# Attention by 64x64 tiles inside an MLP on one core: heads 0 and 2, 1 and 3 put in one tile, states applied in two parts with the scores between them

## The chip, the core and the metric

The kernel runs on one core of one Trainium2 chip. The metric is the device time of one execution in microseconds. TensorE (PE) does the matrix multiplications; each is a weight load (PEld in the profile) and a matmul that streams the other operand past the weights into a bank of PSUM. VectorE (DVE), ScalarE (ACT) and GpSimd (POOL) do elementwise work, and SyncE (SP) issues most of the DMAs.

## The reference

A decayed linear attention over blocks of 64 positions feeds an MLP with a quick GELU. Cut to what matters:

```python
batch, n_heads, seq, head_dim = (4, 8, 768, 64);  block = 64
for b in range(nb):
    intra = np.einsum('bhic,bhjc->bhij', qb, kb) * Dmask[None]       # scores
    intra = np.einsum('bhij,bhjd->bhid', intra, vb)
    inter = np.einsum('bhid,bhde->bhie', qb * lam_pow[None], kv_state)
    out[:, :, sl] = intra + inter                                    # mix
    kv_state = lam_block * kv_state + np.einsum('bhsd,bhse->bhde', kb * rev_pow, vb)
x = out.transpose(0, 2, 1, 3).reshape(B * S, H * D)                  # 3072 x 512
h = x @ w_in                                                         # d_ff 2048
return ((h * (1.0 / (1.0 + np.exp(-1.702 * h)))) @ w_out)            # 3072 x 512, f32
```

## The kernel before

The work is cut into six waves of 512 tokens. Waves 0 and 1 hold the first 256 positions of two batch rows each and are made by separate functions (`big_...`). Waves 2 to 5 hold 128 positions, two blocks of 64, of all four batch rows, and are what the change is about.

Each wave goes through the MLP in 32 items of four 128x512 matmuls each: 16 calls of `mlp1` (line 434, a GELU on ScalarE behind each) and 16 of `mlp2` (line 447), four for each 128 rows of output; a copy (line 451, VectorE) and a store on SyncE follow the fourth. The last 128 rows of the last wave are done by `mlp2_part` (line 458) in column pieces, each with its own copy (line 461) and store.

The order is written out by hand. `main` is the list of MLP items; `side` holds the pieces of attention with the index of the item ahead of which they are issued. While wave w goes through the MLP, the attention of wave w+1 is put between its items, counted from the wave's first item n. Each engine works its own instructions in the order of issue. Attention in waves 2 to 5 goes by pairs of heads p = 0 to 3:

- `load` asks for q, k and v of the wave after next, 24 DMAs of 128 KB on SyncE's queue, at item 8.
- `do_cast` (items 1, 3, 5, 7) multiplies k and q by their powers into a bf16 tile (lines 220 and 221, VectorE), casts v (line 223, GpSimd) and issues a transposing DMA on SyncE's queue (line 226). A tile holds the two heads of a pair, 2p and 2p+1, side by side.
- `scores` (line 376, 64x64 matmuls) for two pairs at once, followed by the mask on VectorE (line 379).
- `state_mm` (line 390, 64x64) and `state_up` (line 399, VectorE): the state after the first block goes to `half_sb`, that after the second to `kv_sb`. Such a state tile is 128x128 for each batch row, with the two heads' 64x64 states on the diagonal and zeros beside them, which `state_zeros` writes on GpSimd.
- `mix` applies the states (line 412, 128x64 matmuls with the block-diagonal state as weights), adds the masked scores times v (line 418, 64x64) and copies the result to xT on ScalarE (line 422). With `then` it also issues scores and states of two other pairs behind its own matmuls.

A 64x64 matmul uses one quarter of the array, a tile set by the half of the input partitions (rows) and the half of the output partitions (columns). `quads` lists the four combinations so that each four neighbours lie on four tiles:

```python
quads = [(r, slice(64 * r, 64 * r + 64), h, slice(64 * h, 64 * h + 64)) for r in range(2) for h in range(2)]
```

PSUM has two groups of banks in this kernel: three of tag "mm" for the MLP and five of tag "att" for attention (`bank`); scores with `spare` take one from "mm". A bank is given out again once its last reader is done.

Of the kernel before, what the change touches and what calls it, by code (L numbers as in the profile page):

```python
# [24 lines left out]
def kernel(  # L25
# [50 lines left out]
    def load(w):  # L76
        for g in range(2):
            for nm in "kqv":
                loaded[w, nm, g] = ld.tile([P, B, 4, D], f32, tag=f"{nm}{g}", name=f"{nm}f")
            for hd in range(4 * g, 4 * g + 4, 2):  # L80
                for nm, src in (("k", k), ("q", q), ("v", v)):
                    for h in (hd, hd + 1):
                        nc.sync.dma_start(
                            out=loaded[w, nm, g][:, :, h % 4, :],
                            in_=src[:, h, w * P : (w + 1) * P, :].rearrange("b s d -> s b d"))
# [84 lines left out]
    def late_pows():  # L170
        for h in range(2):
            hs = slice(64 * h, 64 * h + 64)
            nc.gpsimd.tensor_copy(blk_pow[hs], l64[hs].rearrange("p (n h) -> p n h", h=2)[:, :, h])
        nc.gpsimd.tensor_tensor(blk2_pow, blk_pow, blk_pow, op=MUL)
# [4 lines left out]
    def state_zeros(tiles):  # L179
        for x in tiles:  # L180
            nc.gpsimd.memset(x, 0.0)
# [32 lines left out]
    def do_cast(w, p):  # L214
        kf, qf, vf = (pair_of(w, nm, p) for nm in "kqv")
        kqs = work.tile([P, 2, B, 2, D], bf16, tag=f"kqs{p}", name="kqs")
        ks, qs = kqs[:, 0], kqs[:, 1]
        for h in range(2):
            hd = 2 * p + h
            nc.vector.tensor_scalar(ks[:, :, h, :], kf[:, :, h, :], scalar1=k_pow[:, hd : hd + 1], scalar2=None, op0=MUL)  # L220
            nc.vector.tensor_scalar(qs[:, :, h, :], qf[:, :, h, :], scalar1=q_pow[:, hd : hd + 1], scalar2=None,  # L221
                                    op0=MUL)
        nc.gpsimd.tensor_copy(v_sb[w % 2][p], vf)  # L223
        cast[w, p] = kqs.rearrange("p i b h d -> p i b (h d)")
# [96 lines left out]
    def big_st(w, p0):  # L321
        first, second = part_sb[p0 // 2]
        for i in range(2):
            p = p0 + i
            nc.gpsimd.tensor_scalar(first[:, i], first[:, i], scalar1=blk2_pow[:, p : p + 1], scalar2=None, op0=MUL)  # L325
            for h in range(2):
                hs = slice(64 * h, 64 * h + 64)
                nc.gpsimd.tensor_tensor(kv_sb[0][p][hs, BB * w : BB * w + BB, hs], first[hs, i], second[hs, i], op=ADD)  # L328
# [39 lines left out]
    quads = [(r, slice(64 * r, 64 * r + 64), h, slice(64 * h, 64 * h + 64)) for r in range(2) for h in range(2)]  # L368

    def scores(w, pairs, spare=False):  # L370
        s2 = [bank([P, 2, B, D], f32, "ps_s", spare and h == 0) for h in range(2)]
        for i, p in enumerate(pairs):
            kq = trans[w, p]
            for b in range(B):
                for r, rs, h, hs in quads:
                    nc.tensor.matmul(s2[h][rs, i, b, :], kq[hs, 0, b, rs], kq[hs, 1, b, rs], start=True, stop=True)  # L376
        for h in range(2):
            sm = work.tile([P, 2, B, D], bf16, tag="sm", bufs=8, name="sm")
            nc.vector.tensor_tensor(sm, s2[h], mask_pow[:, pairs[0] : pairs[0] + 2, h, None, :].to_broadcast([P, 2, B, D]),  # L379
                                    op=MUL)  # L380
            masked[w, pairs[0], h] = sm

    def state_mm(w, pairs):
        nr = 2 if w + 1 < NW else 1
        ps_kv = [bank([P, 2, B, D], f32, f"ps_kv{r}") for r in range(nr)]
        for i, p in enumerate(pairs):
            ks, vt = cast[w, p][:, 0], v_sb[w % 2][p]
            for b in range(B):
                for r, rs, h, hs in quads[: 2 * nr]:
                    nc.tensor.matmul(ps_kv[r][hs, i, b, :], ks[rs, b, hs], vt[rs, b, h, :], start=True, stop=True)  # L390
        return ps_kv

    def state_up(w, pairs, ps_kv):
        for r, kv in enumerate(ps_kv):
            for i, p in enumerate(pairs):
                old, new = (kv_sb[w % 2][p], half_sb[p]) if r == 0 else (half_sb[p], kv_sb[(w + 1) % 2][p])
                for h in range(2):
                    hs = slice(64 * h, 64 * h + 64)
                    nc.vector.scalar_tensor_tensor(new[hs, :, hs], old[hs, :, hs], blk_pow[hs, p : p + 1], kv[hs, i],  # L399
                                                   op0=MUL, op1=ADD)  # L400

    def attend(w, pairs):
        scores(w, pairs)
        state_up(w, pairs, state_mm(w, pairs))

    def mix(w, pairs, then=()):
        ps_o = [bank([P, 2, B, D], f32, f"ps_o{r}") for r in range(2)]
        for i, p in enumerate(pairs):
            for r in range(2):
                kv = half_sb[p] if r else kv_sb[w % 2][p]  # L410
                for b in range(B):
                    nc.tensor.matmul(ps_o[r][:, i, b, :], kv[:, b, :], trans[w, p][:, 1, b, r * D : r * D + D],  # L412
                                     start=(i == 0 and b == 0), stop=False, skip_group_check=True)
        for i, p in enumerate(pairs):
            vt = v_sb[w % 2][p]
            for b in range(B):
                for r, rs, h, hs in quads:
                    nc.tensor.matmul(ps_o[r][hs, i, b, :], vt[rs, b, h, :], masked[w, pairs[0], h][rs, i, b, :],  # L418
                                     start=False, stop=True, skip_group_check=True)
# [195 lines left out]
```

## Time and profile before

| | us |
|---|---|
| median of 3 runs | 210.43 (210.26 to 210.76) |
| profiled execution | 210.89 |
| its span in the trace | 209.2 |
| TensorE busy | 199.2 (95%) |
| VectorE busy | 96.8 (46%) |
| ScalarE busy | 86.7 (41%) |
| GpSimd busy | 49.0 (23%) |

Times in the profile are microseconds from the span's start unless ns is written. A group's line gives source line, engine, operation, output and inputs, shape and count, then busy time, mean ns of one, and the idle time of the engine before them with what ended it. A stretch's line gives start and end, its length, the busy time and number of instructions of PE, PEld, DVE, ACT and POOL, TensorE's granted clock, the DMA engines' busy share and GB/s. A timeline line gives start, length, engine, line, operation and count of merged neighbours; in brackets stands idle time before them. A chain line gives start (in the timeline's sense), length and what ran, or only length and share where it is summed.

### The profile page before, as it was taken

How to read it: one execution, taken by the hardware profiler on the slowest of the kernel's cores; microseconds unless marked ns; L12 is line 12 of the kernel's file. 1: busy time of each engine (PE TensorE's matmuls, PEld its weight loads, DVE VectorE, ACT ScalarE, POOL GpSimd, SP SyncE). 2: the span in 40 equal slices, each digit the busy share in tenths (PEclk: the TensorE clock that was granted, in tenths of full speed). 3: DMA queues.
4: the chain of work that ended last, by engine and by line, in shares of the span. 5: the costliest groups of instructions: out<-in, count | busy, mean ns of one | idle time of the engine just before them, and what ended most of it. 6: DMA issues, size and time to landing. Idle time of an engine off the chain costs nothing.

```text
span 209.2 us, 5215 instructions
## 1 busy us (share of the span) xinstructions
PE 199.2 (95%) x2167; PEld 104.6 (50%) x2195; DVE 96.8 (46%) x215; ACT 86.7 (41%) x159; POOL 49.0 (23%) x99
## 2 busy tenths in 40 slices
PE   7979999999999988999999999999999999999993
PEld 7745444555444454444545444545444545444462
DVE  3886000568960399634692725692815251100121
ACT  4539762165766022365212465202466202565000
POOL 4279986183790011200211001111000000000000
PEclk9999999999999999999999999999999999999999
DMA  5999999999999998999993399884490011100112
GB/s 172 267 239 206 198 203 237 297 272 206 189 287 183 201 228 185 279 193 208 209 201 134 90 179 225 183 178 168 98 158 0 34 69 54 50 0 0 53 54 96
DMA packets 88237, 33.89 MB, mean 162 GB/s; under 512 B 68630, under 2 KB 85270, under 8 KB 88214
## 3 DMA queue, kind: packets, MB, share of 16 engines
q1 hardware_dynamic: 83174, 28.98, 60.6%
q0 software_dynamic: 4224, 4.19, 12.4%
q10 hardware_dynamic: 816, 0.39, 0.6%
q8 instruction: 17, 0.28, 0.6%
q14 instruction: 6, 0.05, 0.1%
HBM read 27.26 MB, written 6.29 MB: 160 GB/s over the span
## 4 chain that ended last, share of the span: by engine, by line
PE 83%; DMA 7%; DVE 4%; issue 2%; ACT 2%; ACTq 0%; POOL 0%; POOLq 0%
PE ps_h L434 39%; PE ps_out L447 35%; DMA vb<-in_v_dram 5%; DVE half L399 2%; DMA qb<-in_q_dram 2%; PE ps_part L458 2%; PE ps_o L412 1%; PE ps_o L418 1%; PE ps_s L376 1%; DVE sm L379 1%; DVE kv L399 1%; PE ps_kv L390 1%; ACT mid L315 1%; PE ps_o L348 1%; ACT L555 1%
## 5 line engine op out<-in xcount | busy, mean ns | idle before, releaser
L434 PE MATMUL ps_h<-xT,w_in 128*128 128x512 bf16 x372 | 84.1, 379 | 0.8 <-issue 0.2
L447 PE MATMUL ps_out<-w_out,g_sb 128*128 128x512 bf16 x355 | 80.4, 379 | 1.8 <-issue 1.6
L437 ACT ACTIVATE g_sb<-ps_h 128x512 bf16<-128x512 f32 x96 | 57.1, 598 | 41.8 <-PE ps_h L434 41.7
L434 PEld LDWEIGHTS <-w_in 128*128 128x128 bf16 x384 | 37.1, 98 | 44.5 <-DVE xT L359 0.3
L447 PEld LDWEIGHTS <-g_sb 128*128 128x128 bf16 x368 | 35.0, 98 | 40.6
L451 DVE COPY o_sb<-ps_out 128x512 f32<-128x512 f32 x19 | 13.1, 692 | 55.1 <-PE ps_out L447 53.3
L223 POOL CAST v_sb<-vf 128x512 bf16<-128x512 f32 x16 | 10.1, 638 | 73.2 <-DMA vf<-in_v_dram 62.1
L422 ACT CAST xT<-ps_o 128x512 bf16<-128x512 f32 x16 | 8.6, 590 | 44.0 <-PE ps_o L418 37.4
L379 DVE TENSOR_TENSOR sm<-ps_s,mask_pow 128x512 bf16<-128x512 f32 x16 | 10.3, 686 | 21.5 <-PE ps_s L376 21.4
L399 DVE SCALAR_TENSOR_TENSOR half<-kv,blk_pow,ps_kv 64x256 bf16<-64x256 bf16 x32 | 15.3, 478 | 0.7
L251 DVE TENSOR_TENSOR kqb<-kb,kb_pow 128x256 bf16<-128x256 f32 x10 | 3.9, 422 | 21.4 <-DMA kb<-in_k_dram 19.0
L221 DVE TENSOR_SCALAR kqs<-qf,q_pow 128x256 bf16<-128x256 f32 x32 | 12.6, 395 | 0.8 <-DMA qf<-in_q_dram 0.8
L220 DVE TENSOR_SCALAR kqs<-kf,k_pow 128x256 bf16<-128x256 f32 x32 | 12.1, 377 | 0.5 <-DMA kf<-in_k_dram 0.4
L289 DVE SCALAR_TENSOR_TENSOR smb<-ps_s,inv_pow,mask_b 128x512 bf16<-128x512 f32 x16 | 11.0, 745 | 2.3 <-PE ps_s L281 2.3
L399 DVE SCALAR_TENSOR_TENSOR kv<-half,blk_pow,ps_kv 64x256 bf16<-64x256 bf16 x24 | 11.5, 480 | 0.8
L328 POOL TENSOR_TENSOR kv<-part,part 64x128 bf16<-64x128 f32 x16 | 7.4, 461 | 1.2
L239 PEld LDWEIGHTS <-warm 128*128 128x128 bf16 x79 | 5.8, 127 | 2.0 <-DVE warm L105 1.2
L239 PE MATMUL fill<-warm 128*128 128x64 bf16 (+2 forms) x61 | 5.6, 272 | 1.2 <-DVE warm L105 1.2
L325 POOL TENSOR_SCALAR part<-part,blk_pow 128x128 f32<-128x128 f32 x8 | 5.2, 644 | 5.0 <-ACT part L319 4.4
L268 PEld LDWEIGHTS <-kqb 128*128 128x128 bf16 x64 | 4.5, 105 | 2.8 <-DVE kqb L251 1.5
L451 ACT COPY o_sb<-ps_out 128x512 f32<-128x512 f32 x4 | 2.3, 586 | 8.2 <-PE ps_out L447 8.2
L251 DVE TENSOR_TENSOR kqb<-qb,qb_pow 128x256 bf16<-128x256 f32 x13 | 5.6, 458 | 0.2
(78 smaller groups left out, 123.9 us busy)
## 6 DMA issues: line engine op xcount, KB each, us to landing
out_dram<-o_sb SPq DMA_DIRECT2D x23, 256.0 KB, 2.8
kf<-in_k_dram SPq DMA_DIRECT2D x32, 128.0 KB, 3.4
qf<-in_q_dram SPq DMA_DIRECT2D x32, 128.0 KB, 3.9
vf<-in_v_dram SPq DMA_DIRECT2D x32, 128.0 KB, 3.5
vb<-in_v_dram SPq DMA_DIRECT2D x8, 256.0 KB, 5.5
w_in<-in_moe_w_in_dram POOLq DMA_DIRECT2D x4, 512.0 KB, 9.3
w_out<-in_moe_w_out_dram POOLq DMA_DIRECT2D x4, 512.0 KB, 14.9
kb<-in_k_dram SPq DMA_DIRECT2D x8, 128.0 KB, 3.7
```

Of the source, the lines that this page charges most:

```text
L220: nc.vector.tensor_scalar(ks[:, :, h, :], kf[:, :, h, :], scalar1=k_pow[:, hd : hd + 1], scalar2=None, op0=MUL)
L221: nc.vector.tensor_scalar(qs[:, :, h, :], qf[:, :, h, :], scalar1=q_pow[:, hd : hd + 1], scalar2=None, op0=MUL)
L223: nc.gpsimd.tensor_copy(v_sb[w % 2][p], vf)
L239: nc.tensor.matmul(dst, warm[:, :P], warm[:, : dst.shape[1]], start=True, stop=True, skip_group_check=True)
L251: eng.tensor_tensor(x[:, bb].rearrange("p t (h d) -> p h t d", h=2), pair_of(w, nm, p)[:, bb], by, op=MUL)
L289: nc.vector.scalar_tensor_tensor(sm.rearrange("p b t s -> p b (t s)"), s2.rearrange("p b t s -> p b (t s)"), inv_pow[:, 2 * p + h : 2 * p ...
L379: nc.vector.tensor_tensor(sm, s2[h], mask_pow[:, pairs[0] : pairs[0] + 2, h, None, :].to_broadcast([P, 2, B, D]), op=MUL)
L399: nc.vector.scalar_tensor_tensor(new[hs, :, hs], old[hs, :, hs], blk_pow[hs, p : p + 1], kv[hs, i], op0=MUL, op1=ADD)
L434: nc.tensor.matmul(h_ps[fc], w_in_sb[j][:, kc, i * P : (i + 1) * P], xT[w, kc], start=(kc == 0), stop=(kc == KC - 1))
L437: nc.scalar.activation(g_of[w][:, fc, :], h_ps.pop(fc), GELU)
L447: nc.tensor.matmul(ps_out, g_of[w][:, fc, g * P : (g + 1) * P], w_out_sb[j][:, fc % CW, :], start=(fc == 0), stop=(fc == FFC - 1))
L451: (nc.scalar.copy if w == 0 else nc.vector.tensor_copy)(o, ps_out)
```

## The change

For waves 2 to 5, a tile of q and k now holds heads 0 and 2, or 1 and 3, of a group of four (loads, casts and the powers follow that). A head's v stays where it was. The states become 64 columns wide, without zero blocks: heads 2i+j of a group sit in tile j, partitions 64i to 64i+63; `state_zeros` goes, and a state update covers 128 partitions in one instruction. The states are applied by 64x64 matmuls in two parts: `mix_first` with the two halves of the input partitions writing to swapped banks, `mix_rest` with them straight, followed by the masked scores times v. Between the parts stand the scores and states of two other tiles (`mix_attend`) or four small matmuls of zeros (`mix`); `in_turn` issues one of them. Pieces are placed anew: waves 4 and 5 have their first two pairs cast and scored two MLP waves ahead instead of one, and their loads go out in two halves. The last block's columns go in three pieces of 256, 128 and 128.

```diff
-    def load(w):
-        for g in range(2):
+    def load(w, gs=(0, 1)):
+        for g in gs:
...
-            for hd in range(4 * g, 4 * g + 4, 2):
+            for j in range(2):
                 for nm, src in (("k", k), ("q", q), ("v", v)):
-                    for h in (hd, hd + 1):
+                    for h in ((2 * j, 2 * j + 1) if nm == "v" else (j, j + 2)):
...
-    kv_sb = [[const.tile([P, B, P], bf16, name=f"kv{i}{p}") for p in range(NP)] for i in range(2)]
-    half_sb = [const.tile([P, B, P], bf16, name=f"half{p}") for p in range(NP)]
+    kv_sb = [[const.tile([P, B, D], bf16, name=f"kv{i}{p}") for p in range(NP)] for i in range(2)]
+    half_sb = [const.tile([P, B, D], bf16, name=f"half{p}") for p in range(NP)]
...
+    half_of = [slice(0, D), slice(D, P)]
+    quads = [(i, half_of[i], j, half_of[j]) for i in range(2) for j in range(2)]
+
+    def score_mm(w, p0, spare=False):
         s2 = [bank([P, 2, B, D], f32, "ps_s", spare and h == 0) for h in range(2)]
-        for i, p in enumerate(pairs):
-            kq = trans[w, p]
-            for b in range(B):
-                for r, rs, h, hs in quads:
-                    nc.tensor.matmul(s2[h][rs, i, b, :], kq[hs, 0, b, rs], kq[hs, 1, b, rs], start=True, stop=True)
+        for b in range(B):
+            for r in range(2):
+                for i, rows, j, _ in quads:
+                    kq, rs = trans[w, p0 + j], half_of[r]
+                    nc.tensor.matmul(s2[i][rs, j, b, :], kq[rows, 0, b, rs], kq[rows, 1, b, rs], start=True, stop=True)
...
+    def state_mm(w, p0):
...
+                for r, rs, i, rows in quads[: 2 * nr]:
+                    nc.tensor.matmul(ps_kv[r][rows, j, b, :], cast[w, p0 + j][rs, 0, b, i, :],
+                                     v_sb[w % 2][p0 + i][rs, b, j, :], start=True, stop=True)
...
-                for h in range(2):
-                    hs = slice(64 * h, 64 * h + 64)
-                    nc.vector.scalar_tensor_tensor(new[hs, :, hs], old[hs, :, hs], blk_pow[hs, p : p + 1], kv[hs, i],
-                                                   op0=MUL, op1=ADD)
+                nc.vector.scalar_tensor_tensor(new, old, blk_pow[:, p : p + 1], ps_kv[r][:, j], op0=MUL, op1=ADD)
+
+    def in_turn():
+        nc.tensor.matmul(bank([P, W], f32, "turn")[:D, :D], warm[:D, :D], warm[:D, :D], start=True, stop=True)
...
+    def mix_old(w, p0, swapped):
+        for b in range(B):
+            for i, rows, j, cols in quads:
+                r, p = (1 - i if swapped else i), p0 + j
                 kv = half_sb[p] if r else kv_sb[w % 2][p]
-                for b in range(B):
-                    nc.tensor.matmul(ps_o[r][:, i, b, :], kv[:, b, :], trans[w, p][:, 1, b, r * D : r * D + D],
-                                     start=(i == 0 and b == 0), stop=False, skip_group_check=True)
+                nc.tensor.matmul(mix_of[w, p0][r][cols, i, b, :], kv[rows, b, :], trans[w, p][rows, 1, b, half_of[r]],
+                                 start=(swapped and b == 0), stop=False, skip_group_check=True)
...
+    def mix(w, p0):
+        mix_first(w, p0)
+        for _ in range(4):
+            in_turn()
+        mix_rest(w, p0)
+
+    def mix_attend(w, p0, w2, p2):
+        mix_first(w, p0)
+        in_turn()
+        attend(w2, p2, True)
+        if w2 + 1 == NW:
+            in_turn()
+        mix_rest(w, p0)
...
-                    + [(mlp2_part, w, G - 1, c0, d_model // 2) for c0 in (0, d_model // 2)])
+                    + [(mlp2_part, w, G - 1, c0, n) for c0, n in ((0, 2 * P), (2 * P, P), (3 * P, P))])
...
-                side += [(n + 1 + 2.0 * p, (do_cast, w + 1, p)) for p in range(NP)]
-                at = (21, 25, 28) if w == 1 else (13, 20, 27)
-                side += [(n + at[0], (attend, w + 1, [0, 1])), (n + at[1], (mix, w + 1, [0, 1], (w + 1, [2, 3]))),
-                         (n + at[2], (mix, w + 1, [2, 3]))]
-            if w and w + 2 < NW:
-                side += [(n + 8, (load, w + 2))]
+                p0, ahead = (2 if w > 2 else 0), w > 1 and w + 2 < NW
+                side += [(n + 1 + 2.0 * (p - p0), (do_cast, w + 1, p)) for p in range(p0, NP)]
+                if w < 3:
+                    side += [(n + (20 if w == 1 else 13), (attend, w + 1, 0))]
+                side += [(n + (25 if w == 1 else 18 if w == 2 else 13), (mix_attend, w + 1, 0, w + 1, 2))]
+                if ahead:
+                    side += [(n + (8 if w == 2 else 5), (load, w + 2, (0,))), (n + 21, (load, w + 2, (1,)))]
+                    side += [(n + 15 + 1.5 * p, (do_cast, w + 2, p)) for p in range(2)]
+                    side += [(n + 27, (mix_attend, w + 1, 2, w + 2, 0))]
+                else:
+                    side += [(n + 28, (mix, w + 1, 2))]
+                if w == 1:
+                    side += [(n + 8, (load, w + 2))]
```

Left out here: `do_cast` and `late_pows` index heads and powers by the new places, `big_st` writes its result there, `mix_rest` multiplies the masked scores by v with each four neighbours on four tiles, as before.

More of the change, by code (lines that the diff above doesn't have):

```diff
@@ L416, in mix, with mix_rest @@
+    def mix_rest(w, p0):
+        ps_o = mix_of[w, p0]
+        mix_old(w, p0, False)
+        for i in range(2):
             for b in range(B):
[L417 to L420 removed]
+                for r, rs, j, cols in quads:
+                    nc.tensor.matmul(ps_o[r][cols, i, b, :], v_sb[w % 2][p0 + i][rs, b, j, :],
+                                     masked[w, p0 + i][rs, j, b, :], start=False, stop=True, skip_group_check=True)
+        x = x_tile(w, p0).rearrange("p i (b r s) -> p r (i b) s", b=B, r=2)
@@ L550 @@
         late_mask()
-        state_zeros(kv_sb[0])
         late_pows()
```

75 lines of the change are left out of this document (31 added, 44 removed).

## The prediction

> **What bounds the kernel now.** I read the page first, then the groups of instructions, the stretches (one for each wave of the MLP), and last the timeline of TensorE around the attention pieces.
>
> ```profile
> span 209.2 us, 5215 instructions
> PE 199.2 (95%) x2167; PEld 104.6 (50%) x2195; DVE 96.8 (46%) x215; ACT 86.7 (41%) x159; POOL 49.0 (23%) x99
> ```
>
> ```profile
> L434 PE MATMUL ps_h<-xT,w_in 128*128 128x512 bf16 x372 | 84.1, 379 | 0.8 <-issue 0.2
> L447 PE MATMUL ps_out<-w_out,g_sb 128*128 128x512 bf16 x355 | 80.4, 379 | 1.8 <-issue 1.6
> ```
>
> ```profile
> L434 PEld LDWEIGHTS <-w_in 128*128 128x128 bf16 x384 | 37.1, 98 | 44.5 <-DVE xT L359 0.3 <-issue 0.3
> L447 PEld LDWEIGHTS <-g_sb 128*128 128x128 bf16 x368 | 35.0, 98 | 40.6
> ```
>
> TensorE is busy 95% of the span and no other engine over 46%. The groups also show that the trace lacks records: 384 weight loads stand against 372 matmuls on L434, 368 against 355 on L447. I must allow for that when I read gaps.
>
> ```profile
> 147.28 6.47 PE ps_h L434 x30
> ```
>
> ```profile
> 85.30:116.20 30.90, 30.48 (x349) 15.42 (x352) 17.49 (x40) 11.72 (x20) 3.29 (x5) 1.00 0.86 200
> 116.20:147.10 30.90, 30.48 (x349) 15.40 (x352) 17.13 (x40) 11.71 (x20) 2.46 (x4) 1.00 0.75 171
> 147.10:177.90 30.80, 30.38 (x317) 15.29 (x320) 13.30 (x32) 11.72 (x20) 0.00 (x0) 1.00 0.33 70
> ```
>
> The chain of waits gives the pace of the large matmuls: 6.47/30 = 0.2157 us. A wave has 128 of them, 27.61 us. These three stretches, MLP waves 2 to 4 at full clock (1.00), take 30.90, 30.90 and 30.80 us, so the attention of the next wave adds 3.29, 3.29 and 3.19 us to each on TensorE. That, and the same in wave 1, is all that the change can act on before the tail; work moved on the other engines counts only where TensorE waits for it.
>
> **What one attention piece costs now.** A wave has three: scores and states of heads 0 to 3 (`attend`); the mix of those followed by scores and states of heads 4 to 7; the mix of the latter. In the timeline the first column is the start.
>
> ```profile
> 96.08 0.59 PE L434 MATMUL ps_h<-xT,w_in 128*128 128x512 bf16 x2
> 96.60 0.45 PE L376 MATMUL ps_s<-kqT 64*64 64x64 bf16 x32
> 96.88 0.46 PE L390 MATMUL ps_kv<-v_sb,kqs 64*64 64x64 bf16 x32
> 97.27 0.82 PE L434 MATMUL ps_h<-xT,w_in 128*128 128x512 bf16 x2
> ```
>
> ```profile
> 103.32 0.28 PE L412 MATMUL ps_o<-kqT,kv 128*128 128x64 bf16 x4
> 103.44 0.28 PE L412 MATMUL ps_o<-kqT,half 128*128 128x64 bf16 x4
> ```
>
> ```profile
> 103.88 0.45 PE L418 MATMUL ps_o<-sm,v_sb 64*64 64x64 bf16 x32
> 104.16 0.49 PE L376 MATMUL ps_s<-kqT 64*64 64x64 bf16 x32
> 104.47 0.50 PE L390 MATMUL ps_kv<-v_sb,kqs 64*64 64x64 bf16 x32
> 105.12 0.38 PE L447 MATMUL ps_out<-w_out,g_sb 128*128 128x512 bf16 x1 [0.16 <-issue]
> ```
>
> ```profile
> 111.51 0.45 PE L418 MATMUL ps_o<-sm,v_sb 64*64 64x64 bf16 x32
> 112.11 4.26 PE L447 MATMUL ps_out<-w_out,g_sb 128*128 128x512 bf16 x19 [0.16 <-issue]
> 116.22 1.46 PE L434 MATMUL ps_h<-xT,w_in 128*128 128x512 bf16 x6
> ```
>
> Entry into 64x64 tiles: 96.08 plus two paces is 96.51, and the scores start at 96.60: 0.09 us. Thirty-two small matmuls of which four neighbours lie on four different tiles: 96.60 to 96.88, or 103.88 to 104.16: 0.28 us, 0.035 for each round of four. The way back: five calls, 20 matmuls, stand between 112.11 and 116.22, yet only 19 are recorded, and 4.11/0.2157 is 19, so the first is the missing one and truly started at 111.90. After L418's 0.28 us that leaves 0.11 us, and the "0.16 issue" is no stall. The attend piece agrees: 97.27 - 96.88 = 0.39 = 0.28 + 0.11. L412's sixteen 128x64 matmuls with the switch behind them take 103.88 - 103.32 = 0.56 us, 0.12 for each four (103.44 - 103.32).
>
> So attend costs 0.09 + 0.28 + 0.28 + 0.11 = 0.76, the mix 0.56 + 0.28 + 0.11 = 0.95, the middle piece 0.56 + 3 x 0.28 + 0.11 = 1.51 (1.57 in the rows, with the same missing record). Their sum, 3.22 to 3.28, is the 3.29 of the stretches.
>
> In wave 1 there are stalls besides:
>
> ```profile
> 76.66 0.22 PE L390 MATMUL ps_kv<-v_sb,kqs 64*64 64x64 bf16 x2
> 77.25 0.44 PE L390 MATMUL ps_kv<-v_sb,kqs 64*64 64x64 bf16 x30 [0.38 <-DVE kv L399]
> 77.85 2.54 PE L447 MATMUL ps_out<-w_out,g_sb 128*128 128x512 bf16 x11 [0.16 <-issue]
> ```
>
> ```profile
> 80.46 0.28 PE L412 MATMUL ps_o<-kqT,kv 128*128 128x64 bf16 x4
> 81.22 0.29 PE L412 MATMUL ps_o<-kqT,half 128*128 128x64 bf16 x4 [0.49 <-DVE half L399]
> ```
>
> From 76.66 to 77.25 less a pair's 0.02 is 0.57 us; from 80.46 to 81.22 less 0.12 is 0.64. Wave 1 thus pays 3.29 + 1.21 = 4.50, and all four waves 14.27 us.
>
> **The change, part by part.**
>
> *States applied as 64x64 tiles.* Sixteen 128x64 matmuls and a switch (0.56) become 32 small ones, each four on four tiles: 2 x 0.14 = 0.28. With the entry that a mix did not have (0.09) a mix saves 0.19.
>
> *Scores.* This speaks against the change. In the old loop four neighbours went to four tiles. The new loop nests rows, then input half, then pair, with the output's partitions set by the rows: each two neighbours fall on the same tile, A A B B C C D D. The rows of the old kernel show what one tile can do where the states of the last wave use only two tiles:
>
> ```profile
> 158.71 0.42 PE L390 MATMUL ps_kv<-v_sb,kqs 64*64 64x64 bf16 x16
> 159.06 0.82 PE L434 MATMUL ps_h<-xT,w_in 128*128 128x512 bf16 x2
> ```
>
> 159.06 - 158.71 - 0.11 = 0.24 us for eight pairs: a tile takes a new matmul every 0.030 to 0.035 us however few share the array. If matmuls start in the order of the program, A's second waits one such time, B starts with it, B's second waits again: four times per eight matmuls instead of two. Thirty-two then take 16 x 0.034 = 0.55 us, not 0.28: +0.27 for each of eight score steps, 2.2 us in all. The bounds are 0 (if the engine passed over the waiting one) and, were a second weight load also exposed, twice that. I take 0.27, nearest to the two-tile row.
>
> The Trainium skill, "TensorE: Matmul & The Clock Gate", Part 3 (packing small matmuls), says that matmuls start and end strictly in program order; by it the scores cost the 0.55 and the sum below holds; without it they could cost 0.28 (rival 1). No row here shows it either way.
>
> ```profile
> L390 PE MATMUL ps_kv<-v_sb,kqs 64*64 64x64 bf16 x224 | 3.9, 194 | 0.4 <-DVE kv L399 0.4
> L399 DVE SCALAR_TENSOR_TENSOR half<-kv,blk_pow,ps_kv 64x256 bf16<-64x256 bf16 x32 | 15.3, 478 | 0.7
> L379 DVE TENSOR_TENSOR sm<-ps_s,mask_pow 128x512 bf16<-128x512 f32 x16 | 10.3, 686 | 21.5 <-PE ps_s L376 21.4
> ```
>
> *Fewer pieces, and the turns.* The time between the two halves of a mix is filled by scores and states, or, where there are none, by four `in_turn` matmuls. After the change there are two attends, six joint pieces and two lone mixes: ten visits instead of twelve. Costs: attend 0.09 + 0.55 + 0.28 + 0.11 = 1.03. Joint: 0.09 + 0.14 + 0.03 (one turn) + 0.55 + 0.28 + 0.14 + 0.28 + 0.11 = 1.62 (two of them with half the states, 0.24 + a turn, about the same). Lone mix: 0.09 + 0.14 + 0.14 + 0.28 + 0.11 = 0.76 plus the turns. Four on one tile take 4 x 0.03 = 0.13; but the fourth reuses the first one's bank and waits for its end, 0.19 us after its start by the mean of L390's 64x64 matmuls: 0.25 us with the wait's own time, between 0.13 and 0.8 if every turn waited so. A lone mix is 1.01. Sum: 2 x 1.03 + 6 x 1.62 + 2 x 1.01 = 13.80 us without stalls, against 14.27: -0.47.
>
> *VectorE, and wave 1's stall.* Fifty-six state updates of 64x256 become 28 of 128x256, the same free size, so 0.48 us each: 13 us less of VectorE, off the path in waves 2 to 4. In wave 1 the last mix needs, through a turn's bank, all of two masks and four updates: 2 x 0.69 + 4 x 0.48 = 3.3 us after the scores. The scores now stand ahead of the rest of their own mix, so TensorE has 0.28 + 0.14 + 0.28 + 0.11 of that piece, twelve large matmuls (2.59) and 0.23 of the next piece, 3.6 us, before it asks; the output copy that stood before the masks (the call before) is done by then. So I cost the stall at nothing, with 0.3 us to spare; if that cover goes, up to 1.21 comes back. Next late would be xT's copy, with 16 large matmuls before it is read.
>
> *Moved casts, loads, transposes.* Casts of the wave after next (pairs 0 and 1) go to items 15 and 16.5, half of the loads to item 8 or 5, the other to 21. On SyncE twelve loads now stand ahead of two transposes, and twelve behind one output store. Before, TensorE never waited on these in waves 2 to 4 and VectorE worked 17.5 of 30.9 us. The casts read what was asked for seven items (6 us) before; twelve loads of 128 KB at the stretch's 200 GB/s take 7.9 us, so VectorE may wait some 2 us there with the next masks queued behind. But the states that follow those masks are wanted nine items (7.8 us) after their scores, and masks and updates take 3.3. Cost 0, up to 1 us if loads land later still. The zeroing of twelve state tiles on GpSimd goes; it was waited for nowhere: 0.
>
> *Last block in three.*
>
> ```profile
> 204.05 0.42 DVE L461 COPY o_part<-ps_part 128x256 f32<-128x256 f32 x1 [1.05 <-PE ps_part L458]
> ```
>
> ```profile
> 202.27 3.51 PE ps_part L458 x32
> ```
>
> ```profile
> 46.77 0.22 PE ps_tk L268 x4
> ```
>
> ```profile
> out_dram<-o_sb SPq DMA_DIRECT2D x23, 256.0 KB, 2.8
> out_dram<-o_part SPq DMA_DIRECT2D x2, 128.0 KB, 1.7
> L451 DVE COPY o_sb<-ps_out 128x512 f32<-128x512 f32 x19 | 13.1, 692 | 55.1 <-PE ps_out L447 53.3
> ```
>
> On TensorE 16 x 0.110 (3.51/32) become 32 x 0.055 (0.22/4): nothing. The last copy shrinks: 0.69 for 512 columns, 0.42 for 256, hence 0.29 for 128: -0.13. The last store lands sooner: 2.8 to 1.7 for half the bytes bounds it at 0 to -0.5; I take -0.12. Tail: -0.25.
>
> **Sum.** -0.47 - 0.25 = -0.7 us. The profiled execution took 210.89 us (209.2 span and 1.7 around it), 0.46 above the median of 210.43; so 210.2 for it and 209.7 for the median. About 0.2% (0.42 us) is what a measurement can tell from no change.
>
> **The rivals.**
> (1) The array hides the paired order: scores stay at 0.28. For it: weight loads run ahead. Against: two-tile rows show each tile at its limit, and no row shows a later matmul starting first. -0.7 - 2.2 = -2.9: 207.5.
> (2) Slower: the second of two neighbours on one tile also waits for its weights, because loads into rows in use are not hidden. Place: 128 such followers in the eight score steps; price up to a tile's 0.032 us each, 4.1: 213.8. It decides from 0.7/128 = 0.006 us on. Against: L412's neighbours all use the whole array and still follow at 0.03 (0.12/4), loads hidden. The same section of the Trainium skill states in a list that a load overlaps running matmuls only when its row group differs (the text above the list allows a background weight buffer too); by the list's rule this rival would hold, but the L412 rows, each on the rows of its forerunner, disagree.
> (3) The stall of wave 1 stays (0.3 us is little), or moved loads land late: -0.7 + 1.2 = +0.5: 210.9.
>
> **How the numbers follow.** Forecast 58%, rival 1 14%, rival 2 14%, rival 3 14%. The forecast's own range: the pair's time between 0.030 and 0.035 (+-0.3), turns and tail (+-0.3): 209.1 to 210.4; it is faster by over 0.2% in most of it, 50 of its 58. With rival 1's 14: 0.64. Same: 8 of the forecast, 4 of rival 3: 0.12. Slower: rival 2 and the rest of rival 3: 0.24. The range, 207.3 to 211.0, takes in rivals 1 and 3 and leaves out rival 2.
>
> **What would show it.** Scores of 32 taking 0.55 (0.28: rival 1; 0.8 or more: rival 2); 64x64 state rows of 0.14 per 16; waves 3 and 4 at about 30.8 and 30.2 us, wave 2 longer, near 31.9, since it gets a third piece; no releaser "DVE" before TensorE in wave 1 (rival 3 if there); a last copy of 0.29. Waves 2 to 4 all above 31 would make the prediction wrong.

## The result, and the profile after

The changed kernel takes 209.17 us (median of seven runs), the kernel before beside it 210.76 (seven runs): ratio 0.9913, 95% interval 0.9886 to 0.9940, so 1.8 us less (1.3 to 2.4). The ratio is one of means and leaves out one execution of the changed kernel, of 213.72 us, that fell in a slower state. On record stood a forecast of -0.7 (209.7, range 207.3 to 211.0) and, as rival 1, -2.9. The result is faster, as forecast, and lies halfway between the two, so some term of the sum must be wrong. The profiled execution took 209.56 us.

Two lines of the page (the profile's summary) after:

```profile
span 207.9 us, 5498 instructions
PE 198.2 (95%) x2327; PEld 102.3 (49%) x2355; DVE 82.2 (40%) x188; ACT 86.5 (42%) x159; POOL 45.2 (22%) x88
```

VectorE lost 14.6 us of work (96.8 before) and GpSimd 3.8; TensorE is as full as it was. The stretches of MLP waves 2 to 4 of the changed kernel, from each wave's first weight load to the next one's:

```profile
84.89:116.25 31.36, 30.94 (x448) 15.57 (x451) 17.55 (x46) 11.70 (x20) 4.69 (x5) 1.00 0.96 200
116.25:146.66 30.41, 30.09 (x369) 14.83 (x372) 12.27 (x30) 11.61 (x20) 2.74 (x5) 1.00 0.86 197
146.66:176.67 30.01, 29.80 (x308) 14.31 (x311) 6.94 (x16) 11.61 (x20) 0.62 (x1) 1.00 0.21 59
```

They were forecast at near 31.9, 30.8 and 30.2, against 30.9, 30.9 and 30.8 before. Now one attend piece of wave 2:

```profile
95.24 1.24 PE L451 MATMUL ps_h<-xT,w_in 128*128 128x512 bf16 x5
96.42 0.46 PE L377 MATMUL ps_s<-kqT 64*64 64x64 bf16 x32
96.69 0.48 PE L389 MATMUL ps_kv<-v_sb,kqs 64*64 64x64 bf16 x32
97.11 1.04 PE L451 MATMUL ps_h<-xT,w_in 128*128 128x512 bf16 x3
```

The scores take 96.42 to 96.69, 0.27 us, where 0.55 was forecast: rival 1's sign. The joint piece of wave 3, which has half the states, shows how it can be (a count of x1 stands for single matmuls):

```profile
141.74 0.41 PE L389 MATMUL ps_kv<-v_sb,kqs 64*64 64x64 bf16 x14
141.96 0.22 PE L411 MATMUL ps_o<-kqT,half 64*64 64x64 bf16 x2
141.98 0.20 PE L389 MATMUL ps_kv<-v_sb,kqs 64*64 64x64 bf16 x2
142.01 0.19 PE L411 MATMUL ps_o<-kqT,half 64*64 64x64 bf16 x1
142.01 0.19 PE L398 MATMUL turn<-warm 64*64 64x64 bf16 x1
...
142.10 0.19 PE L424 MATMUL ps_o<-sm,v_sb 64*64 64x64 bf16 x1
142.11 0.19 PE L411 MATMUL ps_o<-kqT,kv 64*64 64x64 bf16 x1
```

In the program all sixteen L389 come first, then the turn (L398), then all L411 of `mix_rest`, then L424. In the trace two L411 start at 141.96, ahead of the last L389 at 141.98 and of the turn at 142.01, and an L424 at 142.10 ahead of an L411 at 142.11. The states here are those of the last wave and use one half of the input partitions; the L411 that pass them, those of `half`, use the other. TensorE lets a later small matmul on a free tile start before an earlier one that waits.

Could the program itself stand in another order than the source? The kernel sets its order by hand (`tc.manual_schedule()`), and the same calls in wave 4 run in a slightly different one, with thirteen L389 ahead of the two L411 instead of fourteen:

```profile
158.65 0.38 PE L389 MATMUL ps_kv<-v_sb,kqs 64*64 64x64 bf16 x13
158.84 0.22 PE L411 MATMUL ps_o<-kqT,half 64*64 64x64 bf16 x2
```

The table gives what the pieces cost, each as the time from the start of the last large matmul ahead to that of the first one behind, less the pace of 0.2157 us for each (the missing record behind a piece allowed for):

| us | before | forecast | after |
|---|---|---|---|
| attend | 0.76 | 1.03 | 0.785 |
| joint piece, waves 1 and 2 | 2.12 (stalled) and 1.58 | 1.62 | 1.47 |
| joint piece, waves 3 and 4 | 1.50 to 1.56 | 1.62 | 1.34 to 1.43 |
| lone mix, wave 4 | 0.95 | 1.01 | 1.01 |
| lone mix, wave 1 | 1.61 | 1.01 | 1.21 |
| all of waves 1 to 4 | 14.23 | 13.80 | 12.34 |
| last matmul to the end | 3.41 | 3.16 | 3.10 |

Pieces and tail together are 2.2 us less. The span is only 1.3 less, because the first large matmul (its weight load) started at 19.42 instead of 18.58. Nothing ties that to the change: in the other profiles this start lies between 18.03 and 19.71 whichever kernel it is, the old order's own at 18.41, 18.58 and 19.71.

### The profile page after: what moved, and what is told of

It is laid out like the page before. It is cut to its first block, busy times and chain, and to the rows that moved or that the text cites. A ratio compares the mean times of both kernels' runs of the same rounds, so it can differ in the third digit from the quotient of the medians.

```text
span 207.9 us, 5498 instructions
## 1 busy us (share of the span) xinstructions
PE 198.2 (95%) x2327; PEld 102.3 (49%) x2355; DVE 82.2 (40%) x188; ACT 86.5 (42%) x159; POOL 45.2 (22%) x88
## 4 chain that ended last, share of the span: by engine, by line
PE 87%; DMA 7%; ACT 2%; issue 1%; SPq 0%; POOL 0%; ACTq 0%; DVE 0%; POOLq 0%
PE ps_h L451 39%; PE ps_out L464 38%; DMA vb<-in_v_dram 5%; PE ps_part L475 2%; DMA qb<-in_q_dram 2%; PE ps_o L411 2%; PE ps_o L424 1%; PE ps_s L377 1%; PE ps_kv L389 1%; ACT mid L314 1%; PE ps_o L348 1%; ACT L571 1%; PE ps_kv L307 1%; PE ps_s L280 1%; PE ps_tq L267 0%
## 5 line engine op out<-in xcount | busy, mean ns | idle before, releaser
L222 POOL CAST v_sb<-vf 128x512 bf16<-128x512 f32 x16 | 11.7, 740 | 74.9 <-DMA vf<-in_v_dram 74.8
L395 DVE SCALAR_TENSOR_TENSOR half<-kv,blk_pow,ps_kv 128x256 bf16<-128x256 bf16 x16 | 6.9, 473 | 0.0
L250 DVE TENSOR_TENSOR kqb<-qb,qb_pow 128x256 bf16<-128x256 f32 x13 | 6.2, 504 | 0.1
L267 PEld LDWEIGHTS <-kqb 128*128 128x128 bf16 x64 | 4.0, 98 | 3.7 <-DVE kqb L250 2.6
L268 ACT COPY kqB<-ps_tq 128x512 bf16<-128x512 bf16 x6 | 3.5, 586 | 5.1 <-PE ps_tq L267 5.1
## 6 DMA issues: line engine op xcount, KB each, us to landing
w_out<-in_moe_w_out_dram POOLq DMA_DIRECT2D x4, 512.0 KB, 14.6
```

The source lines that it names most:

```text
L222: nc.gpsimd.tensor_copy(v_sb[w % 2][p], pair_of(w, "v", p))
L250: eng.tensor_tensor(x[:, bb].rearrange("p t (h d) -> p h t d", h=2), pair_of(w, nm, p)[:, bb], by, op=MUL)
```

## The experiments

Each ratio is to the kernel before on the same chip, with its 95% interval. The cost of a piece is read from the run's profile as in the table above. For all four orders of the score loop: eight score steps lie in the pieces, and the rest of the kernel is the changed one.

### The order of the scores on the tiles

**Four neighbours on four tiles (s_four).**

```diff
-        for b in range(B):
-            for r in range(2):
-                for i, rows, j, _ in quads:
...
+        for b in range(B):
+            for j in range(2):
+                for r in range(2):
+                    for i in range(2):
...
```

> The changed kernel with the score loop nested so that each four neighbours lie on four tiles, as in the old kernel; nothing else differs. Theory A (mine on record: matmuls start in order, and a tile takes one per 0.032 us) needs the paired order to cost 0.55 us for 32 scores; the new trace already shows the first 32 in 0.27, so A is in trouble, and if its records' starts hid a cost this kernel would be 2 us faster than the changed one. Theory B (the array takes two matmuls per half of its rows every 0.032 us, whichever columns they use): no difference, 0.27 to 0.28 us for 32 scores, total within 0.3 us of the changed kernel.

Measured: ratio 0.9914 (0.9883 to 0.9945), attend 0.762 against 0.785. The paired order costs 0.02 in an attend piece, nothing in the joint pieces (1.47 in both) and nothing that the time can tell. Going back to the old kernel's order of tiles brings nothing, so nothing was lost by leaving it.

**Sixteen on one row half (s_half).**

```diff
+        for i in range(2):
+            for b in range(B):
+                for j in range(2):
+                    for r in range(2):
...
```

> The changed kernel with the score loop's outermost index the half of the input partitions: 16 scores in a row on one half of the rows, alternating between its two tiles, then 16 on the other. Theory A (one matmul per tile per 0.032 us): 16 pairs of 0.032, 0.51 us for 32 scores instead of 0.27, so 8 x 0.24 = 1.9 us slower than the changed kernel. Theory B (two per row half per 0.032): the same 0.51 us and +1.9 us. Theory C (only the rate of issue, about 0.008 us for each matmul, sets the pace): 0.27 us and no difference.

**Eight on one tile (s_tile).**

```diff
+        for i in range(2):
+            for r in range(2):
+                for b in range(B):
+                    for j in range(2):
...
```

> The changed kernel with 8 scores in a row on the same tile, tile after tile. Theory A (one per tile per 0.032 us, in order): 32 x 0.032 = 1.0 us for 32 scores, 8 x 0.75 = 6 us slower than the changed kernel. Theory B (two per row half per 0.032 us whichever columns): 0.51 us, 1.9 us slower. Theory C (issue alone): no difference.

Measured: s_half 0.9949 (0.9922 to 0.9976), attend 0.874, that is +0.11 over s_four; s_tile 1.0039 (1.0011 to 1.0068), attend 1.174, +0.41, and the whole of the change's gain is lost by a loop order alone. None of the three theories fits: over s_four's, all pieces together cost 0.57 us more in s_half (on record 1.9 or nothing) and 2.97 in s_tile (on record 6, 1.9 or nothing). In s_tile's attend:

```profile
96.79 0.80 PE L378 MATMUL ps_s<-kqT 64*64 64x64 bf16 x29
97.40 0.22 PE L390 MATMUL ps_kv<-v_sb,kqs 64*64 64x64 bf16 x3
97.43 0.19 PE L378 MATMUL ps_s<-kqT 64*64 64x64 bf16 x1
97.45 0.20 PE L390 MATMUL ps_kv<-v_sb,kqs 64*64 64x64 bf16 x2
...
97.49 0.19 PE L378 MATMUL ps_s<-kqT 64*64 64x64 bf16 x1
```

The states, which stand behind all scores in the program, start at 97.40, before the scores are through. In strict order, four runs of eight on one tile would take at least four times seven steps of 0.032, 0.90 us, from first to last start, and the states would follow; the last score starts at 97.49, 0.70 us after the first, with some of the states already under way.

**Four on one tile (s_quad).**

```diff
+        for b2 in range(0, B, 2):
+            for r in range(2):
+                for i in range(2):
+                    for b in (b2, b2 + 1):
+                        for j in range(2):
...
```

> The changed kernel, with the score loop so that each four neighbours fall on one tile (A A A A B B B B C C C C D D D D, twice). Measured so far per attend piece over four neighbours on four tiles (0.762): pairs on one tile +0.02, sixteen on one row half +0.11, eight on one tile +0.41. Theory one, strict order of the program with 0.032 us for each follower on a tile: +0.57 per piece, eight pieces 4.6 us, ratio 1.013. Theory two, TensorE looks past a waiting matmul at about the next four: +0.12 per piece (worked out step by step with one start in 0.008 us and 0.032 us per tile), 1.0 in all, ratio 0.996. Theory three, it looks past eight or more: +0.03 or less, ratio 0.991 to 0.992.

Measured: 0.9947 (0.9917 to 0.9977), attend 0.832, +0.07; the joint pieces rose by 0.04. Strict order (+0.57) is refuted. How many matmuls TensorE looks past is not settled. An estimate worked out step by step, with one start in 0.008 us (0.27/32) and 0.032 us between two on one tile, gives 0, 0.03, 0.13 and 0.19 for pairs, fours, a row half and eights with a look-ahead of eight, and 0, 0.13, 0.19 and 0.38 with one of four; measured are 0.02, 0.07, 0.11 and 0.41. What limits the look-ahead stays open.

### Where the gain comes from

**Same tiles, old number of pieces (n_ahead).**

```diff
...
+                side += [(n + 1 + 2.0 * p, (do_cast, w + 1, p)) for p in range(NP)]
+                at = (20, 25, 28) if w == 1 else (13, 20, 27)
+                side += [(n + at[0], (attend, w + 1, 0)), (n + at[1], (mix_attend, w + 1, 0, w + 1, 2)),
+                         (n + at[2], (mix, w + 1, 2))]
+            if w and w + 2 < NW:
+                side += [(n + 8, (load, w + 2))]
```

> The changed kernel, but with the pieces of attention placed as the old order has them: in each of MLP waves 1 to 4 one attend, one joint piece and one lone mix, casts at items 1, 3, 5, 7 and loads at item 8. Twelve visits to the small tiles instead of ten; tiles, states and tail as in the changed kernel. If the gain comes from the pieces themselves (entry, switch and turns, which a merged visit saves), then by the changed kernel's pieces (attend 0.785, joint 1.36 to 1.47, lone mix 1.01) waves 3 and 4 add 3.2 each instead of 2.77 and 2.36, wave 2 3.25 instead of 3.72: pieces 13.0 instead of 12.34, about 0.7 to 0.8 slower than the changed kernel, ratio to the kernel before 0.995. Rival: the merging is worth nothing, since a lone mix with its turns only fills time that the joint piece spends as well, and all of the gain is in the states applied as 64x64 tiles: ratio 0.991, as the changed kernel. Second rival: the early casts and halved loads of the changed kernel cost something that the records hide; then this one is as fast or faster, ratio 0.990 or less.

Measured: 0.9949 (0.9924 to 0.9974), pieces 13.15. Waves 2 to 4:

```profile
83.51:114.49 30.98, 30.53 (x387) 15.10 (x390) 12.57 (x32) 11.70 (x20) 5.69 (x6) 1.00 0.91 211
114.49:145.40 30.91, 30.46 (x387) 14.97 (x390) 12.57 (x32) 11.70 (x20) 2.46 (x4) 1.00 0.88 172
145.40:176.12 30.72, 30.30 (x355) 14.87 (x358) 11.01 (x28) 11.70 (x20) 0.00 (x0) 1.00 0.33 70
```

These are the old kernel's 30.90, 30.90 and 30.80. So the 64x64 states by themselves bring nothing here: what a joint piece saves by them (1.47 against 1.58), a lone mix gives back with its four turns (1.07 against 0.95). The merging of pieces brings 13.15 - 12.34 = 0.81 us by the profiles, about as worked out on record (0.7 to 0.8); the timed intervals of the two kernels overlap.

**The old kernel, wave 1's pieces moved (b_early).**

```diff
-                at = (21, 25, 28) if w == 1 else (13, 20, 27)
+                at = (20, 25, 30) if w == 1 else (13, 20, 27)
```

> The kernel before, with only wave 1's pieces placed differently: attend one item earlier (20 instead of 21) and the lone mix two items later (30 instead of 28). It asks how much of the changed kernel's gain is the two stalls behind VectorE in wave 1 (0.57 in the joint piece, 0.64 in the lone mix, 1.21 in all), which the old tiles could have lost too. Theory one: both stalls go, joint 1.51 to 1.57 instead of 2.12, lone mix 0.95 instead of 1.61, wave 1 33.1 instead of 34.28, gain 1.2, ratio 0.994. Theory two: attend an item earlier waits for its transposes, or the mix two items later lets the next wave wait for xT: the stall moves, ratio 1.000.

Measured: 0.9946 (0.9915 to 0.9977). Wave 1 of the kernel before, then of this one:

```profile
50.79:85.07 34.28, 32.24 (x422) 16.38 (x420) 22.12 (x45) 13.89 (x27) 10.81 (x19) 1.00 1.03 211
```

```profile
51.66:84.74 33.08, 31.90 (x421) 16.29 (x420) 22.39 (x45) 13.88 (x27) 10.20 (x18) 1.00 1.02 210
```

Both stalls are gone, 1.20 us, as in theory one; pieces 13.04, the same as the new tiles without merging (13.15, of which 0.11 is the stall of the next part: its lone mix in wave 1 cost 1.187, not 1.073). Two numbers changed in the old kernel give about as much as all of the new tiles in the old places.

**Updates split in halves again (u_split)**, on the kernel of f_shift below.

```diff
-                nc.vector.scalar_tensor_tensor(new, old, blk_pow[:, p : p + 1], ps_kv[r][:, j], op0=MUL, op1=ADD)
+                for hs in half_of:
+                    nc.vector.scalar_tensor_tensor(new[hs], old[hs], blk_pow[hs, p : p + 1], ps_kv[r][hs, j], op0=MUL, op1=ADD)
```

> The changed kernel with TensorE's instructions shifted by 32 places (thirty-two 64-column fillers at the start, as in the run before, ratio 0.9875), and besides with every state update split again into its two halves of 64 partitions: 56 updates of 64x256 instead of 28 of 128x256, some 13 us more of VectorE. It asks what hides VectorE in wave 1. In the changed kernel the updates end at 80.0 and the lone mix asks at about 80.8. Theory one, the cover of wave 1 is 0.3 to 0.8 us: four more updates at 0.39 in the joint piece end 1.6 later, and the lone mix of wave 1 costs 1.9 instead of 1.07, with VectorE as the releaser; waves 2 to 4 as they were; 0.8 slower than the shifted kernel, ratio 0.991. Theory two, the cover is larger (the turns don't need all updates): nothing changes, ratio 0.9875. Theory three, VectorE's 13 us count elsewhere too, since masks and casts are queued behind the updates: waves 2 to 4 longer than 31.36, 30.41, 30.01, ratio above 0.993.

Measured: 1.0039 (1.0006 to 1.0072), 3.4 us slower than f_shift by the medians. That is far beyond theory one's 0.991, and past the bound of theory three, but not for its reason: waves 2, 3 and 4 went only from 31.36, 30.41 and 30.01 to 31.66, 30.57 and 30.02. In wave 1 the joint piece costs 2.01 (1.47 in f_shift) and the lone mix 3.06 (1.07), 2.5 us together; the first of wave 2's joint pieces costs 1.76. The waits and the timeline:

```profile
PE turn L399 <- DVE kv L396: 1.8, 1, 1.8
...
PE ps_kv L389 <- DVE kv L396: 0.4, 1, 0.4
```

```profile
82.68 0.19 PE L399 MATMUL turn<-warm 64*64 64x64 bf16 x1 [1.83 <-DVE kv L396]
...
83.49 5.08 PE L465 MATMUL ps_out<-w_out,g_sb 128*128 128x512 bf16 x15 [0.16 <-issue]
```

The turn waits 1.83 us for the last update, as the prediction's step said a turn would. In this profile fifteen large matmuls then take 5.08 us where fifteen at full clock take 3.40 (the kernel before, from 82.05): the granted clock fell (its column is the one after the five engines):

```profile
82.60:84.00 1.40, 1.16 (x52) 0.88 (x53) 0.72 (x2) 0.58 (x2) 0.00 (x0) 0.81 1.04 231
84.00:86.00 2.00, 2.00 (x6) 0.65 (x5) 0.00 (x0) 0.50 (x2) 0.61 (x1) 0.50 0.96 208
86.00:88.00 2.00, 2.00 (x9) 0.81 (x8) 0.00 (x0) 0.00 (x0) 0.39 (x1) 0.78 1.11 369
```

That is 1.7 us more, but not in every execution: the mean granted clock was 0.992 in four of the twelve, the profiled one among them (213.08 to 213.37 us), and 1.00 in the other eight (210.88 to 212.46). Two of 29 executions of the kernel before, whose stalls are 0.57 and 0.64 us, had 0.992 too. So the one instruction per update is needed in wave 1 and hardly anywhere else. That the wait of some 2 us brought the clock down is likely from its place right behind the wait, but not shown.

### The stall in wave 1's lone mix

In the changed kernel this mix costs 1.21 to 1.79 in different profiles where it should cost 1.07. Seen best in the profile of t_two, below:

```profile
80.75 0.20 PE L411 MATMUL ps_o<-kqT,half 64*64 64x64 bf16 x2
81.46 0.22 PE L411 MATMUL ps_o<-kqT,kv 64*64 64x64 bf16 x2 [0.52 <-issue]
```

```profile
79.27 0.87 DVE L395 SCALAR_TENSOR_TENSOR kv<-half,blk_pow,ps_kv 128x256 bf16<-128x256 bf16 x2
```

TensorE stops after the tenth matmul of the piece, its weight loads too, while VectorE's last update ended at 80.14, 0.6 before the stop. The releaser reads "issue": no semaphore that the profile shows. The profile's DMA queues (packets, MB, share) include one of kind "instruction":

```profile
q8 instruction: 18, 0.29, 0.6%
```

These are packets of 16 KB. The changed kernel has 18 of them and 2355 weight loads with a matmul each, one packet for 262 of TensorE's instructions; the kernel before has 17 and 2195, one for 258. So they are read here as blocks of TensorE's program. In the packet records of t_two one was fetched from 79.06 to 80.08; TensorE went on 1.38 later. In the profiles of the changed kernel and of s_four the block ended at 79.24 and 78.84, and TensorE went on 1.51 and 1.56 later.

**The mix one item later (m29).**

```diff
-                    side += [(n + 28, (mix, w + 1, 2))]
+                    side += [(n + (29 if w == 1 else 28), (mix, w + 1, 2))]
```

> The changed kernel, with the lone mix of MLP wave 1 one item later (29 instead of 28). In five profiles that mix stalls after its tenth matmul by 0.15 to 0.73 us, weight loads too. Theory one, TensorE's own instructions: they come in blocks of 16 KB by the instruction queue, a block was fetched 2.5 us before the stall ends, and TensorE goes on 1.4 to 1.6 us after the packet's end. With 0.86 us more of large matmuls between, the fetch is over in time: no stall, lone mix 1.05 instead of 1.21 (up to 1.79). Theory two, VectorE (masks and updates of the joint piece, done at 80.0 where TensorE went on at 80.75): also no stall, so this run alone does not tell them apart. Theory three, something inside the lone mix itself (the banks of its turns): the stall stays, 0.15 to 0.7. By the first two the kernel gains 0.15 to 0.6 on the changed one, ratio 0.989; by the third nothing.

**TensorE's instructions shifted by 32 places (f_shift).**

```diff
-        fill(f0, 16, P)
+        fill(f0, 32, 64)
```

> The changed kernel, but the first filler matmuls of the program, sixteen of 128 columns on zeros, become thirty-two of 64 columns: the same time on TensorE at the start, and every later instruction of TensorE (a weight load and a matmul count as two) stands 32 places further. Nothing else moves: the order and the distance of the lone mix of wave 1 from VectorE's updates are as in the changed kernel. Theory one, blocks of TensorE's instructions: the block's border goes from the tenth matmul of the lone mix to the large matmuls ahead of it, where a late block is covered by queued work of 0.2 us each: no stall at the tenth matmul, lone mix about 1.05. Theory two, VectorE: the stall stays where it is, 0.15 to 0.7 after the tenth matmul. Theory three, banks of the turns: stays too. Time 209.0 by the first, 209.2 by the others; the time cannot tell them, the records can.

Measured: m29 0.9873 (0.9844 to 0.9903), f_shift 0.9875 (0.9840 to 0.9909); the lone mix costs 1.07 in both, without a stall, which refutes the third theory. The intervals overlap the changed kernel's, so the profiles decide. In f_shift VectorE's updates and the mix keep their places to each other:

```profile
78.22 0.86 DVE L395 SCALAR_TENSOR_TENSOR kv<-half,blk_pow,ps_kv 128x256 bf16<-128x256 bf16 x2
```

```profile
79.69 0.20 PE L411 MATMUL ps_o<-kqT,half 64*64 64x64 bf16 x2
79.69 0.20 PE L411 MATMUL ps_o<-kqT,kv 64*64 64x64 bf16 x2
79.72 0.20 PE L411 MATMUL ps_o<-kqT,half 64*64 64x64 bf16 x2
79.72 0.20 PE L411 MATMUL ps_o<-kqT,kv 64*64 64x64 bf16 x2
```

The last update ends at 79.08 and the piece runs through its tenth matmul. The blocks now come at 73.50, ahead of the joint piece, and from 78.80 to 79.84, with no stop behind it. Only the place of the instructions in their blocks had changed, so VectorE and the turns' banks are out, and TensorE's own supply of instructions is what is left. What makes it fetch early or late was not tried.

### The last block

**Two pieces again (t_two).**

```diff
-                    + [(mlp2_part, w, G - 1, c0, n) for c0, n in ((0, 2 * P), (2 * P, P), (3 * P, P))])
+                    + [(mlp2_part, w, G - 1, c0, n) for c0, n in ((0, 2 * P), (2 * P, 2 * P))])
```

> The changed kernel with its last block in two pieces of 256 columns, as before. On record for three pieces: -0.13 for the copy and -0.12 for the store. If that is right this kernel is 0.25 us slower than the changed one, and the time from TensorE's last matmul to the span's end goes back from 3.10 to 3.40 us. If the end were set elsewhere: no difference.

**Three pieces in the kernel before (b_tail).**

```diff
-                    + [(mlp2_part, w, G - 1, c0, d_model // 2) for c0 in (0, d_model // 2)])
+                    + [(mlp2_part, w, G - 1, c0, n) for c0, n in ((0, 2 * P), (2 * P, P), (3 * P, P))])
```

> The kernel before, with only the last block in three pieces of 256, 128 and 128 columns instead of two of 256. On record: a gain of 0.25, copy -0.13 and store -0.12. The changed kernel with two pieces had 3.42 us from the last matmul to the end, with three 3.10. Expected here 3.41 to 3.10, ratio 0.9985 (0.31 of 211). Rival: two more instructions on SyncE and VectorE or a third group on TensorE eat it: ratio 1.000. Its profile also gives a second sample of when the first large matmul of the old order starts (18.58 in the one before).

**Four pieces, on f_shift (best).**

```diff
-                    + [(mlp2_part, w, G - 1, c0, n) for c0, n in ((0, 2 * P), (2 * P, P), (3 * P, P))])
+                    + [(mlp2_part, w, G - 1, c0, n) for c0, n in ((0, 2 * P), (2 * P, P), (3 * P, D), (3 * P + D, D))])
```

> The changed kernel with TensorE's instructions shifted by 32 places (ratio 0.9875 before) and the last block in four pieces of 256, 128, 64 and 64 columns instead of three. Last copy 0.29 to about 0.22 (0.42 for 256, 0.29 for 128), last store half the bytes again: tail 3.12 to about 3.0, on TensorE nothing if 64 columns take half of 128's 0.055. Ratio 0.987. Rival: the small matmuls or one more store eat it: tail 3.1, part 3.7 to 3.9 long, ratio 0.988.

Measured from the last matmul to the end: two pieces 3.41 (before) and 3.42 (t_two), three 3.10 (after) and 3.11 (b_tail), four 2.92. Ratios: t_two 0.9927 (0.9896 to 0.9958), b_tail 0.9979 (0.9950 to 1.0008), best 0.9883 (0.9848 to 0.9917). The times can't tell a tail's 0.3 us; the profiles can. The last copies, of the kernel after and of best:

```profile
204.79 0.29 DVE L478 COPY o_part<-ps_part 128x128 f32<-128x128 f32 x1 [0.60 <-PE ps_part L475]
```

```profile
204.49 0.22 DVE L478 COPY o_part<-ps_part 128x64 f32<-128x64 f32 x1 [0.24 <-PE ps_part L475]
```

The fourth piece takes 0.2 off the tail (3.12 in f_shift), and TensorE's part of the last block grows by 0.04 (3.70 to 3.74). Best is 208.62 us, f_shift 208.73, m29 208.5: each below the changed kernel's 209.17 by its median, with overlapping intervals, and not told apart from each other. The tail of best is a little shorter than the 3.0 on record.

## Why the prediction was right, and where it was not

The sign and the range were right, but the largest term of the sum was wrong. What came true for the scores is rival 1, which had 14%; the stated range of 207.3 to 211.0 was drawn to hold that rival too. That 209.17 lies even in the forecast's own range (209.1 to 210.4) is luck: beside it the kernel before took 210.76 and not the 210.43 that the sum started from, and three terms priced too low gave back 0.70 of the 2.16 that the scores were priced too high. The sum of the pieces was 13.80 on record and is 12.34. Term by term:

*Scores: wrong.* The step "if matmuls start in the order of the program" failed. It added 2.16 us (eight times 0.27); the paired order costs 0.02 in an attend piece, 0.2 at most in eight. The row on which it rested, two-tile states of the last wave, showed the limit of a tile and not the order of starts: nothing stood behind those states that could have passed them. The Trainium skill, "TensorE: Matmul & The Clock Gate", Part 3 (packing small matmuls), says that matmuls start strictly in program order; the rows at 141.96 and 97.40 show later ones starting first, and the measurement decides. The rule in its list that a load overlaps only where the row group differs would have made rival 2 true; s_quad, with 24 of each 32 scores behind one on their own tile, costs 0.07, where rival 2 allowed up to 0.8 (24 x 0.032).

*Joint pieces: 0.1 too low.* With scores of 0.28 the working would have given 1.35; waves 1 and 2 measure 1.47. The masked scores times v in the joint piece of wave 2, then in a lone mix:

```profile
102.43 0.53 PE L424 MATMUL ps_o<-sm,v_sb 64*64 64x64 bf16 x32
```

```profile
173.06 0.43 PE L424 MATMUL ps_o<-sm,v_sb 64*64 64x64 bf16 x32
```

Less the 0.19 of the last, the same thirty-two start in 0.34 us at the end of 129 small matmuls and in 0.24 at the end of 68. They are slower at the end of the long piece; why wasn't tried. The four joint pieces with full states cost 0.44 us more than 1.35 each, which offset a part of the first error.

*States and turns: right.* The lone mix of wave 4 costs 1.01 as worked out, so also the 0.25 of the turns.

*VectorE and wave 1's stall: right on VectorE, not foreseen otherwise.* In the changed kernel's wave 1:

```profile
79.14 0.87 DVE L395 SCALAR_TENSOR_TENSOR kv<-half,blk_pow,ps_kv 128x256 bf16<-128x256 bf16 x2
```

```profile
80.81 0.47 PE L398 MATMUL turn<-warm 64*64 64x64 bf16 x4
```

VectorE's updates end at 80.01, the turns start at 80.81, 0.14 of it by the new stall: the 0.3 to spare was about 0.65, and no wait on VectorE is left. But the other stall, of 0.14 here and up to 0.72 in other profiles, took its place, by the supply of instructions. That no profile of before showed such a stall is why no rival had it.

*Loads, casts and transposes: right.* Nothing in waves 2 to 4 waits on them. *Last block: right*, 0.31 for 0.25.

Together: 2.16 too much by the scores, and 0.44 (joint), 0.20 (wave 1's lone mix) and 0.06 (attends) too little, 1.46 in all: 13.80 to 12.34. The 2.2 us that the profiles show are 1.07 in wave 1 (1.21 of stalls on VectorE, less 0.14 of the new one), 0.81 in merged pieces and 0.31 in the tail; the timed 1.8 (1.3 to 2.4) holds that.

## What to carry to other kernels

Four neighbours on four tiles is a good order but not a law: here pairs on one tile were hidden, eights were not, so look for a row in which something could have passed the waiting instruction before pricing a strict order. A stall is first priced as one that moving a call by an item or two may remove (1.2 us here, by two numbers in the old kernel). After packing many small matmuls together, look for stalls without a semaphore, and at where the packets of the instruction queue fall.

## What the runs showed of the hardware

- TensorE starts small matmuls out of program order where an earlier one's tile is busy (141.96 ahead of 141.98 in the changed kernel); a row of eight on one tile is beyond what it hides (+0.41 us for 32).
- TensorE's program comes in blocks of 16 KB while it runs (18 packets for 4710 instructions). Where a lone mix of 68 small matmuls started 4 us behind the start of a joint piece of 129, TensorE stood still for 0.11 (n_ahead) to 0.72 us (t_two); with the instructions shifted by 32 places it did not.
- Behind 1.83 us of waiting in u_split's profile the granted clock stood at 0.50: 5.08 us for fifteen large matmuls that take 3.40 at full clock. The mean granted clock shows such a loss in four of twelve executions. The Trainium skill, "TensorE: Matmul & The Clock Gate", Part 1, gives an idle window of about 3.4 us as what returns the clock to half; here TensorE's longest gap between starts was 2.0 us (to 82.68), with no other above 0.63 within ten us of it, so in this execution less was enough. The stall of 0.72 in t_two left the clock at 1.00.
